# The front of a fused FNet and ELU kernel: first batch loaded tile by tile, two folds on GpSimd, and the channel-128 rows moved to earlier steps

## The chip, the cores and the metric

One NeuronCore of a Trainium2 chip runs the kernel. The metric is device time in microseconds for one execution, lower is better; the figures of the kernel before are three runs and one profiled execution.

## The reference

```python
def _attn_ref(x):                      # x: (8, 3008, 256) float32
    X = np.fft.fft(x, axis=1)
    X = np.fft.fft(X, axis=2)
    return X.real.astype(np.float32)

def _moe_ref(x, w_in, w_out):          # x: (24064, 256), w_in: (256, 2048), w_out: (2048, 256)
    h = x @ w_in
    g = np.where(h > 0.0, h, np.exp(np.minimum(h, 0.0)) - 1.0)
    return (g @ w_out).astype(np.float32)
```

The output of the first feeds the second. The two weight matrices arrive as 64-bit floats, so the kernel converts them itself.

## The kernel before, in words

**The sequence transform.** A batch is four tiles `xl0` to `xl3` of 128 rows by six blocks of 256 channels: `xl0` and `xl3` hold rows in rising order, `xl1` and `xl2` mirrored rows. Each is filled half by gathers that GpSimd issues (`gather`) and half by plain DMAs in SP's queue (`ahead`, `back`). `fold_x` adds and subtracts mirrored channels (`e0` to `e3`, `o0` to `o3`), then mirrored rows (`E0`, `E2`, `O0`, `O2`, `EO0` to `EO3`, `S`/`D`). DFT matrices `MC` turn the folded tiles into four half transforms of a batch (R and I, even and odd), which VectorE unfolds and joins into the rings `Rr` and `Ir`. Rings and the later stages work in column tiles of 256; there are 47 of them.

**The layers.** For each column tile there are eight steps, so 376 in all, of `PERIOD` = 4.8 model units. Step s does P (`mm_P`: `Wc` by `Rr`), V (`even_part`: VectorE adds the outer product of row `Rb` and column `wex`), Q (`mm_Q`: `Ws` by `Ir`), then h, the relu and exp on ScalarE (b+, b-, x+, x-) and g+, g- on VectorE. Two steps later the products with `w_out` follow: directly (`mm_plain`) for the first 16 steps, and from step 16 as seven products on sums that GpSimd makes (`sum_1` to `sum_4`). Finished tiles are combined, transposed on VectorE (`turn_u`, `turn_v`) and stored by SP in many small DMAs (`store`, L1199). All of an engine's compute runs in the order of its instructions, so an engine that waits holds up what stands behind it.

**Weights.** `w1_chunks` and `w2_chunks` are loaded raw and converted by steps named in the schedule (`w0a`, `w0b`, `w0R` and so on, on VectorE, ScalarE and GpSimd). `fold_chunk` (`f0`) turns a chunk of `w_in` into `Wc` and `Ws`. For chunks 2 to 7 the last row of `Ws` is written to DRAM (`wx`, L525) and read back as the columns `wex` (L528), both by SP.

**Channel 128.** It pairs with no other channel, so its rows come apart. Batch 0 takes them from the loaded tiles (`fold_first`, `dft_ext_0`); for all eight batches at once, `load_ext` fetches single elements (16 calls, L809), `sort_ext` orders them on ScalarE, `xe_dr` and `get_ext` (L839, L844) take them through DRAM into the tile `xs`, `fold_ext` folds them on GpSimd, and `dft_ext` transforms them. `ext_side` copies the results to SBUF, `ext_unfold` and `ext_rows` unfold and join them, and DMAs write them to DRAM, whence `spread_ext` brings them into `Rb` and into row 127 of `Ir`.

**The order.** Every piece of work is an event `at(t, fn)`. Events are sorted by time and traced in that order; instructions that go through `pin` keep it on their engine, other DMAs are placed by the framework's scheduler. The list `FRONT` gives the events of the start by name.

Of the kernel before, what the change touches and what calls it, by code (L numbers as in the profile page):

```python
# [9 lines left out]
FP = mybir.dt.float32  # L10
# [5 lines left out]
ALU = mybir.AluOpType  # L16
# [5 lines left out]
HALF = SEQ // 2  # L22
# [3 lines left out]
NE = 377  # L26
NO = 376
NA = (95, 94)
# [102 lines left out]
def kernel(  # L131
# [313 lines left out]
    def load_mats(ri, kodd, cuts=()):  # L445
        n = OFF[2 * ri + kodd]
        ends = (0, *cuts, BW[kodd])
        for a, z in zip(ends, ends[1:]):
            nc.sync.dma_start(
                out=MC[ri, kodd][:, a:z], in_=MC_dr.ap()[:, n + a : n + z]  # L450
            )
# [29 lines left out]
    def vtt(o, a, b, op):  # L481
        pin(nc.vector.tensor_tensor(out=o, in0=a, in1=b, op=op))  # L482
# [214 lines left out]
    def steps_of(pos, n, step):  # L697
        stop = pos + (n - 1) * step + (1 if step > 0 else -1)
        return slice(pos, stop if stop >= 0 else None, step)
# [7 lines left out]
            yield steps_of(pos, m, step), i, i + m  # L707
            i += m

    def unfold(es, even, near, ab, ri, kodd, M, tt):  # L710


        na, nc_ = NA[kodd], NC[kodd]
        n = NO if kodd else NE
        a, c = even[0:M, 0:na], even[0:M, 2 * na : 2 * na + nc_]
        b, ab = near[0:M, 0:na], ab[0:M]
        tt(ab[:, 0:na], a, b, ALU.add)
        p, q = (b, a) if ri else (a, b)
        tt(ab[:, steps_of(nc_ - 1, 94, -1)], p[:, 0:94], q[:, 0:94], ALU.subtract)
        tt(es[0:M, 0:nc_], ab[:, 0:nc_], c, ALU.add)  # L720
        p, q = (c, ab) if ri else (ab, c)
        tt(es[0:M, steps_of(n - 1, 188, -1)], p[:, 0:188], q[:, 0:188], ALU.subtract)

    def join(es, odd, kodd, to, tt, ri=0, part=None):


        def put(up, at, n, step, e, o):
            for sl, i, z in to(at, n, step):
                u, v = (e, o) if up or not ri else (o, e)
                tt(sl, u(i, z), v(i, z), ALU.add if up else ALU.subtract)  # L730

        def run(t, start, step):
            return lambda i, z: t[:, steps_of(start + i * step, z - i, step)]

        base, top = kodd * RUN, kodd * RUN + RUN - 1
        for up in (True, False):
            if part not in (None, up):
                continue
            if kodd:
                put(up, base if up else top, NO, 1 if up else -1, run(es, 0, 1), run(odd, 0, 1))  # L740
                continue
            for h in range(2):
                first = h if up or h else 2
                n = (189, 188)[h] if up else (187, 188)[h]
                put(
                    up,
                    base + first if up else top - first + 1,
                    n,
                    2 if up else -2,
                    run(es, first, 2),  # L750
                    run(odd, 189 * h + first // 2, 1),
                )

    class Dft:
# [21 lines left out]
        def unfold(self):  # L776
            self.es = spool.tile([128, NE], FP, tag="bs", bufs=3, name="bs")
            ab = spool.tile([128, 189], FP, tag="ab", bufs=2, name="ab")
            unfold(self.es, self.even, self.near, ab, self.ri, self.kodd, self.M, vtt)

        def to(self, at, n, step):
            for sl, i, z in ring_cut(self.b * HALF + at, n, step):
# [99 lines left out]
    def ext_side(g, rows=NB):  # L882
        kodd, par = EXT[g]
        n = (NO if kodd else NE) if par else 2 * NA[kodd] + NC[kodd]
        t = spool.tile([128, 380], FP, tag="side", bufs=2, name="side")
        act(t[0:rows, 0:n], state["ext"][32 * g : 32 * g + rows, 0:n])
        state["side", par] = t

    def ext_unfold(kodd, tt, rows=NB):
        even = state["side", 0]  # L890
        a = spool.tile([128, NE], FP, tag="bs", bufs=3, name="bs")
        ab = spool.tile([128, 189], FP, tag="ab", bufs=2, name="ab")
        unfold(a, even, even[:, NA[kodd] : 2 * NA[kodd]], ab, 0, kodd, rows, tt)
        state["es"] = a[0:rows]

    def ext_rows(kodd, tt, rows=NB):
        if not kodd or rows < NB:
            rx = spool.tile([128, HALF + 1], FP, tag="rx", bufs=1, name="rx")
            state["rx"] = rx[0:rows]
        rx, a, b = state["rx"], state["es"], state["side", 1][0:rows]  # L900
        base = kodd * RUN

        def to(at, n, step):
            yield rx[:, steps_of(at, n, step)], 0, n

        join(a, b, kodd, to, tt)
        if not kodd:
            tt(rx[:, HALF:], a[:, 0:1], b[:, 0:1], ALU.subtract)
            nc.sync.dma_start(
                out=r4_dr.rearrange("o b -> b o"), in_=rx[:, HALF : HALF + 1]  # L910
            )
        nc.sync.dma_start(
            out=r128_dr[0:rows, base : base + RUN], in_=rx[:, base : base + RUN]
        )

    def spread_ext(b, kodd):
        for sl, a, z in ring_cut(b * HALF + kodd * RUN, RUN, 1):
            a, z = a + kodd * RUN, z + kodd * RUN
            nc.sync.dma_start(
                out=Rb[:, sl],  # L920
                in_=r128_dr[b : b + 1, a:z].to_broadcast([128, z - a]),
            )
            nc.sync.dma_start(out=Ir[127:128, sl], in_=r128_dr[b : b + 1, a:z])
# [68 lines left out]
    def exp_neg(ap):  # L992
        act(ap, ap, func=AF.Exp, scale=-1.0)
# [273 lines left out]
    L_first, loads = load_x(0)  # L1267
    row_table(1)
    loads[0]()
    loads[6]()  # L1270
    w1_chunks[0].load()
    row_table(0)
    row_table(2)
    for load in loads[1:6] + loads[7:]:
        load()
    row_table(3)
    exp_neg(warm)
    nc.sync.dma_start(out=CC, in_=CC_dr.ap())
    load_mats(0, 0, (663,))
    w1_chunks[1].load()  # L1280
    nc.sync.dma_start(out=pick, in_=PK_dr.ap())
    EO, ops = fold_x(
        L_first,
        lambda key: nc.vector,
        lambda key, n: (0, 4, n) if key in ("e0", "e2") else (0, n),
    )

    def dft_now(d, par, tag):
# [7 lines left out]
    def at(t, fn):  # L1296
        events.append((t, len(events), fn))


    def load_rest():  # L1300

        ops["x1", 0]()
        act(MC[1, 0][0:1, 0:1], L_first[1][0:1, 0:1])
        load_mats(1, 0)
        w2_chunks[0].load()
        w1_chunks[2].load()
        load_mats(0, 1)
        for chunk in (w1_chunks[3], w2_chunks[1], w1_chunks[4], w2_chunks[2]):
            chunk.load()
        load_mats(1, 1)  # L1310
        w1_chunks[5].load()
        w2_chunks[5].load()
# [21 lines left out]
        ("R4", R_even.half),  # L1334
    )}
    for (key, i) in list(ops):
        names[key + "ab"[i] if key in ("e0", "e2") else key] = ops[key, i]
    for c in range(6):
        for name, chunk in ((f"w{c}", w1_chunks[c]), (f"u{c}", w2_chunks[c])):
            for key, fn in zip(  # L1340
# [26 lines left out]
    for slot in range(8):  # L1367
# [7 lines left out]
            names[f"{key}{slot}"] = lambda fn=fn, i=i: fn(i)  # L1375

    FRONT = (
        (-20.84, "e3 o3"),
        (-19.11, "w0a w0b w0p w0R c3"),
        (-17.62, "w0s w0M"),  # L1380
        (-16.21, "e0a e2b o2"),
        (-14.32, "e2a o0 c2"),
        (-12.89, "E2 f0 O2"),
        (-11.63, "xl1 xs e1 x-even"),
        (-9.8, "e0b c1 o1 c0 x-odd x-copy Wc0"),
        (-8.58, "E0 Ws0 EO0 S0 D0"),
        (-7.29, "wm0 wex0 O0 R-odd"),
        (-5.76, "w1b EO2 S2 D2"),
        (-4.55, "w2b R-even u0b w2d u0a EO1 w1d"),
        (-3.25, "I-odd R-copy w1l w1a x-sum u0l"),  # L1390
        (-1.92, "w1R R-sum w1p I-even x-down R-up"),
        (-0.64, "Irc2 w1s u0p P0 x-up I-copy w1M"),
        (0.82, "R-down O-even Irc I-sum u1l V0"),
        (2.21, "w1P w2l P1 I-up u0d"),
        (3.48, "I-down Q0 u0R R4 V1"),
        (4.76, "f1 h0 b+0 O-copy u0s Q1"),
        (5.99, "x+0 w2a b-0 u0M O-odd"),
        (7.24, "Wc1 g+0 x-0 O-sum Ws1"),
# [159 lines left out]
    at(9 * T + 4.75, dft_ext_0)  # L1558
    for g in (2, 3):
        at(10 * T + 1.46, lambda g=g: ext_side(g, 1))  # L1560
    at(11 * T + 3.54, lambda: ext_unfold(1, gtt, 1))
    at(11 * T + 3.55, lambda: ext_rows(1, gtt, 1))
    at(11 * T + 3.6, lambda: spread_ext(0, 1))
    for n in range(16):
        at((10.2 + 0.7 * n) * T, lambda n=n: load_ext(*divmod(n, 4)))
    at(24 * T + 1.5, sort_ext)
    at(26 * T, get_ext)
    at(32 * T + 1.35, fold_ext)
    at(32 * T + 4.75, dft_ext)
    at(33 * T + 1.46, lambda: ext_side(0))  # L1570
    at(33 * T + 1.47, lambda: ext_side(1))
    at(35 * T + 0.2, lambda: ext_unfold(0, vtt))
    at(35 * T + 1.5, lambda: ext_rows(0, vtt))
    at(35 * T + 4.75, lambda: ext_side(2))
    at(35 * T + 4.76, lambda: ext_side(3))
    at(36 * T + 0.2, lambda: ext_unfold(1, vtt))
    at(36 * T + 1.5, lambda: ext_rows(1, vtt))
    fold_keys = [(k, p) for k in FOLDS for p in range(2 if k[0] not in "cxSD" else 1)]
    n_big = sum(k[0] not in "cxSD" for k, _ in fold_keys)
    for b in range(1, NB):  # L1580
# [82 lines left out]
```

## Time and profile before

| what | value |
|---|---|
| median of 3 runs | 1961.19 us (1960.39 to 1961.99) |
| profiled execution, its own time | 1964.17 us |
| its span | 1962.4 us |
| mean granted TensorE clock | 0.994 |
| TensorE, VectorE, ScalarE, GpSimd busy | 98%, 67%, 44%, 72% |
| instructions | 27279 |
| DMA | 262111 packets, 69.70 MB, 245375 packets under 512 B |

TensorE (PE) is nearly always busy. The useful views are therefore those of its few idle stretches: what it waited for, and what its feeder was doing. In a line of the time line the first two figures are the start and the busy time in microseconds; `xN` merges N instructions, and a bracket gives the idle time before and what ended it. Merged lines give no single duration.

### The profile page before, as it was taken

To read this page: it belongs to the slowest core of one execution; us is meant where nothing else is said; L and a number is where in the kernel's file an instruction comes from. 1 tells how busy PE (TensorE), PEld (TensorE's weight loads), DVE (VectorE), ACT (ScalarE), POOL (GpSimd) and SP (SyncE) were. 2 spreads that over 40 slices of the span, in tenths; PEclk is the share of its full clock that TensorE was granted. 3 is DMA by queue.
4 is the path that set the end of the run, shared out by engine and by line. 5 is a ranking of instruction groups with operands and counts; after the bars stand their busy time and mean duration, and the time that the engine had idled before them with its cause. 6 is when DMAs were issued, how large, how long until landed. Compare 5 with 4: busy or idle time off the path is not lost.

```text
span 1962.4 us, 27279 instructions
## 1 busy us (share of the span) xinstructions
PE 1929.7 (98%) x8912; PEld 1655.8 (84%) x8912; DVE 1310.3 (67%) x2517; ACT 864.3 (44%) x1678; POOL 1403.9 (72%) x1868
## 2 busy tenths in 40 slices
PE   7899999999999999999999999999999999999998
PEld 4678878888888888888888888888888888888887
DVE  7766676667666666666666666666666666667665
ACT  3554434444444444444444444444434444344443
POOL 3687767777677776787677776778767787456565
PEclk9999999999999999999999999999999999999999
DMA  9244121120111112011110102102020110100101
GB/s 287 75 21 48 22 55 21 26 47 16 45 18 34 33 23 49 15 40 23 30 43 20 38 18 45 28 19 51 13 49 17 20 20 16 17 11 12 22 11 23
DMA packets 262111, 69.70 MB, mean 36 GB/s; under 512 B 245375, under 2 KB 246291, under 8 KB 261969
## 3 DMA queue, kind: packets, MB, share of 16 engines
q1 hardware_dynamic: 255952, 55.11, 15.1%
q0 software_dynamic: 3840, 12.59, 2.1%
q8 instruction: 71, 1.16, 0.3%
q14 instruction: 72, 0.58, 0.1%
q10 hardware_dynamic: 2176, 0.26, 0.1%
HBM read 43.07 MB, written 24.80 MB: 35 GB/s over the span
## 4 chain that ended last, share of the span: by engine, by line
PE 93%; DVE 4%; DMA 1%; POOL 1%; issue 1%; SPq 0%; ACT 0%; DVEq 0%; POOLq 0%
PE H L476 37%; PE pB L476 16%; PE pC L476 16%; PE pD L476 16%; PE pA L476 8%; DVE E L968 1%; DVE G L998 1%; POOL G L485 0%; DMA xl<-in_x_dram 0%; DMA CC<-chan_mats 0%; DVE v L482 0%; DVE bs L482 0%; DVE e L573 0%; DMA wex<-wx 0%; DVE u L482 0%
## 5 line engine op out<-in xcount | busy, mean ns | idle before, releaser
L485 POOL TENSOR_TENSOR G<-G 128x256 f32<-128x256 f32 x1440 | 1036.8, 730 | 486.3 <-DVE G L998 378.1
L968 DVE SCALAR_TENSOR_TENSOR E<-Rb,wex,H 128x256 f32<-128x256 f32 x752 | 327.8, 477 | 535.7 <-PE H L476 521.1
L488 ACT ACTIVATE G<-H 128x512 f32<-128x512 f32 x376 | 224.6, 597 | 971.8 <-DVE G L982 961.1
L476 PE MATMUL H<-Ir,Ws 128*128 128x256 f32 x1504 | 390.0, 382 | 13.1 <-DVE E L968 12.2
L476 PE MATMUL H<-Rr,Wc 128*128 128x256 f32 x1504 | 387.6, 380 | 2.0 <-DVE Ir L482 1.4
L476 PE MATMUL pC<-G,WT 128*128 128x256 f32 x1440 | 370.4, 380 | 0.0
L476 PEld LDWEIGHTS H<-Ir,Ws 128*128 128x128 f32 x1504 | 279.2, 190 | 63.5 <-DVE E L968 17.7
L476 PEld LDWEIGHTS H<-Rr,Wc 128*128 128x128 f32 x1504 | 285.0, 190 | 53.0 <-issue 4.5
L476 PEld LDWEIGHTS pC<-G,WT 128*128 128x128 f32 x1440 | 274.2, 190 | 37.5
L982 DVE SCALAR_TENSOR_TENSOR G<-E,H 128x512 f32<-128x512 f32 x376 | 256.8, 683 | 43.2 <-POOL G L485 3.8
L998 DVE SCALAR_TENSOR_TENSOR G<-G,H 128x512 f32<-128x512 f32 x376 | 255.8, 680 | 43.5 <-ACT G L488 43.4
L998 DVE SCALAR_TENSOR_TENSOR G<-M,G 128x512 f32<-128x512 f32 x376 | 256.7, 683 | 1.6 <-ACT M L488 1.6
L488 ACT ACTIVATE G<-G 128x512 f32<-128x512 f32 x376 | 233.2, 620 | 0.0
L476 PE MATMUL pB<-G,w 128*128 128x256 f32 x784 | 232.5, 384 | 0.0
L476 PE MATMUL pD<-G,w 128*128 128x256 f32 x784 | 229.4, 379 | 0.0
L476 PE MATMUL pA<-G,w 128*128 128x256 f32 x784 | 229.3, 379 | 0.0
L488 ACT ACTIVATE M<-G 128x512 f32<-128x512 f32 x376 | 223.9, 596 | 3.3 <-DVE G L982 3.3
L488 ACT ACTIVATE M<-M 128x512 f32<-128x512 f32 x376 | 220.9, 588 | 0.1
L476 PE MATMUL pB<-G,WT 128*128 128x256 f32 x720 | 215.2, 380 | 1.0 <-POOL G L485 0.7
L476 PE MATMUL pD<-G,WT 128*128 128x256 f32 x720 | 214.7, 380 | 0.0
L476 PEld LDWEIGHTS pB<-G,w 128*128 128x128 f32 x784 | 151.3, 193 | 21.3
L476 PEld LDWEIGHTS pD<-G,w 128*128 128x128 f32 x784 | 149.2, 190 | 20.4
(170 smaller groups left out, 1442.3 us busy)
## 6 DMA issues: line engine op xcount, KB each, us to landing
out_dram<-ot SPq DMA_DIRECT2D x496, 32.0 KB
xl<-in_x_dram SPq DMA_DIRECT2D x16, 256.0 KB
xl<-in_x_dram SPq DMA_DIRECT2D x32, 128.0 KB
out_dram<-ot SPq DMA_DIRECT2D x256, 2.0 KB
Rb<-r SPq DMA_DIRECT2D x10, 376.0 KB
raw<-in_moe_w_in_dram SPq DMA_DIRECT2D x7, 512.0 KB
raw<-in_moe_w_out_dram SPq DMA_DIRECT2D x4, 512.0 KB
out_dram<-ot SPq DMA_DIRECT2D x64, 28.0 KB
```

The source lines that it names most:

```text
L476: nc.tensor.matmul(out_, lhsT=lhsT, rhs=rhs, start=start, stop=stop, skip_group_check=True)
L485: pin(nc.gpsimd.tensor_tensor(out=o, in0=a, in1=b, op=op))
L488: pin(nc.scalar.activation(out=o, in_=i, func=func, **kw))
L968: nc.vector.scalar_tensor_tensor(out=S.E[:, c], in0=Rb[:, cols(i)], scalar=wex[:, f : f + 1], in1=S.H[:, c], op0=ALU.mult, op1=ALU.add,)
L982: nc.vector.scalar_tensor_tensor(out=two(S.G[:, 0:512])[:, :, ::-1], in0=two(S.E), scalar=2.0, in1=two(S.H), op0=ALU.mult, op1=ALU.subtract,)
L998: nc.vector.scalar_tensor_tensor(out=o, in0=e, scalar=-1.0, in1=h, op0=ALU.add, op1=ALU.max)
```

## The change

Six edits. The first batch's SP loads are issued tile after tile; the first chunk of `w_in` is loaded behind the tiles, the DFT matrices and `CC`, and the second chunk with the rest. The folds `o1` and `O0` of batch 0 go to GpSimd, and the folds `e0` and `e2` are no longer cut in two. The first 18 lines of `FRONT` become ten with another order. Unfolding channel 128 is split into `unfold_near` and `unfold_far` and joining into up and down, each an event in a step of its own; batch 0's goes from GpSimd to VectorE. The channel-128 data is loaded at a closer spacing and sorted, fetched, folded and transformed in steps 18 to 20 instead of 24 to 32. The odd half's sides share one tile (`sides`), so that they last until steps 29 to 32.

```diff
--- before.py
+++ after.py
@@ -707,16 +707,19 @@
             yield steps_of(pos, m, step), i, i + m
             i += m
 
-    def unfold(es, even, near, ab, ri, kodd, M, tt):
+    def unfold_near(even, near, ab, ri, kodd, M, tt):
 
 
         na, nc_ = NA[kodd], NC[kodd]
-        n = NO if kodd else NE
-        a, c = even[0:M, 0:na], even[0:M, 2 * na : 2 * na + nc_]
-        b, ab = near[0:M, 0:na], ab[0:M]
+        a, b, ab = even[0:M, 0:na], near[0:M, 0:na], ab[0:M]
         tt(ab[:, 0:na], a, b, ALU.add)
         p, q = (b, a) if ri else (a, b)
         tt(ab[:, steps_of(nc_ - 1, 94, -1)], p[:, 0:94], q[:, 0:94], ALU.subtract)
+
+    def unfold_far(es, even, ab, ri, kodd, M, tt):
+        na, nc_ = NA[kodd], NC[kodd]
+        n = NO if kodd else NE
+        c, ab = even[0:M, 2 * na : 2 * na + nc_], ab[0:M]
         tt(es[0:M, 0:nc_], ab[:, 0:nc_], c, ALU.add)
         p, q = (c, ab) if ri else (ab, c)
         tt(es[0:M, steps_of(n - 1, 188, -1)], p[:, 0:188], q[:, 0:188], ALU.subtract)
@@ -776,7 +779,8 @@
         def unfold(self):
             self.es = spool.tile([128, NE], FP, tag="bs", bufs=3, name="bs")
             ab = spool.tile([128, 189], FP, tag="ab", bufs=2, name="ab")
-            unfold(self.es, self.even, self.near, ab, self.ri, self.kodd, self.M, vtt)
+            unfold_near(self.even, self.near, ab, self.ri, self.kodd, self.M, vtt)
+            unfold_far(self.es, self.even, ab, self.ri, self.kodd, self.M, vtt)
 
         def to(self, at, n, step):
             for sl, i, z in ring_cut(self.b * HALF + at, n, step):
@@ -882,30 +886,42 @@
     def ext_side(g, rows=NB):
         kodd, par = EXT[g]
         n = (NO if kodd else NE) if par else 2 * NA[kodd] + NC[kodd]
-        t = spool.tile([128, 380], FP, tag="side", bufs=2, name="side")
+        if not kodd or rows < NB:
+            t = spool.tile([128, 380], FP, tag="side", bufs=2, name="side")
+        else:
+            if not par:
+                state["sides"] = spool.tile([128, 776], FP, tag="xn", bufs=1, name="sides")
+            t = state["sides"][:, 380 * par : 380 * par + 380]
         act(t[0:rows, 0:n], state["ext"][32 * g : 32 * g + rows, 0:n])
-        state["side", par] = t
-
-    def ext_unfold(kodd, tt, rows=NB):
-        even = state["side", 0]
+        state["side", kodd, par] = t
+
+    def ext_near(kodd, rows=NB):
+        even = state["side", kodd, 0]
+        state["ab"] = spool.tile([128, 189], FP, tag="ab", bufs=2, name="ab")
+        unfold_near(
+            even, even[:, NA[kodd] : 2 * NA[kodd]], state["ab"], 0, kodd, rows, vtt
+        )
+
+    def ext_far(kodd, rows=NB):
         a = spool.tile([128, NE], FP, tag="bs", bufs=3, name="bs")
-        ab = spool.tile([128, 189], FP, tag="ab", bufs=2, name="ab")
-        unfold(a, even, even[:, NA[kodd] : 2 * NA[kodd]], ab, 0, kodd, rows, tt)
+        unfold_far(a, state["side", kodd, 0], state["ab"], 0, kodd, rows, vtt)
         state["es"] = a[0:rows]
 
-    def ext_rows(kodd, tt, rows=NB):
-        if not kodd or rows < NB:
+    def ext_rows(kodd, up, rows=NB):
+        if up and (not kodd or rows < NB):
             rx = spool.tile([128, HALF + 1], FP, tag="rx", bufs=1, name="rx")
             state["rx"] = rx[0:rows]
-        rx, a, b = state["rx"], state["es"], state["side", 1][0:rows]
+        rx, a, b = state["rx"], state["es"], state["side", kodd, 1][0:rows]
         base = kodd * RUN
 
         def to(at, n, step):
             yield rx[:, steps_of(at, n, step)], 0, n
 
-        join(a, b, kodd, to, tt)
+        join(a, b, kodd, to, vtt, 0, up)
+        if up:
+            return
         if not kodd:
-            tt(rx[:, HALF:], a[:, 0:1], b[:, 0:1], ALU.subtract)
+            vtt(rx[:, HALF:], a[:, 0:1], b[:, 0:1], ALU.subtract)
             nc.sync.dma_start(
                 out=r4_dr.rearrange("o b -> b o"), in_=rx[:, HALF : HALF + 1]
             )
@@ -1267,22 +1283,20 @@
     L_first, loads = load_x(0)
     row_table(1)
     loads[0]()
-    loads[6]()
-    w1_chunks[0].load()
     row_table(0)
     row_table(2)
-    for load in loads[1:6] + loads[7:]:
+    for load in loads[1:]:
         load()
     row_table(3)
     exp_neg(warm)
+    load_mats(0, 0, (663,))
     nc.sync.dma_start(out=CC, in_=CC_dr.ap())
-    load_mats(0, 0, (663,))
-    w1_chunks[1].load()
+    w1_chunks[0].load()
     nc.sync.dma_start(out=pick, in_=PK_dr.ap())
     EO, ops = fold_x(
         L_first,
-        lambda key: nc.vector,
-        lambda key, n: (0, 4, n) if key in ("e0", "e2") else (0, n),
+        lambda key: nc.gpsimd if key in ("o1", "O0") else nc.vector,
+        lambda key, n: (0, n),
     )
 
     def dft_now(d, par, tag):
@@ -1302,6 +1316,7 @@
         ops["x1", 0]()
         act(MC[1, 0][0:1, 0:1], L_first[1][0:1, 0:1])
         load_mats(1, 0)
+        w1_chunks[1].load()
         w2_chunks[0].load()
         w1_chunks[2].load()
         load_mats(0, 1)
@@ -1334,7 +1349,7 @@
         ("R4", R_even.half),
     )}
     for (key, i) in list(ops):
-        names[key + "ab"[i] if key in ("e0", "e2") else key] = ops[key, i]
+        names[key] = ops[key, i]
     for c in range(6):
         for name, chunk in ((f"w{c}", w1_chunks[c]), (f"u{c}", w2_chunks[c])):
             for key, fn in zip(
@@ -1375,24 +1390,16 @@
             names[f"{key}{slot}"] = lambda fn=fn, i=i: fn(i)
 
     FRONT = (
-        (-20.84, "e3 o3"),
-        (-19.11, "w0a w0b w0p w0R c3"),
-        (-17.62, "w0s w0M"),
-        (-16.21, "e0a e2b o2"),
-        (-14.32, "e2a o0 c2"),
-        (-12.89, "E2 f0 O2"),
-        (-11.63, "xl1 xs e1 x-even"),
-        (-9.8, "e0b c1 o1 c0 x-odd x-copy Wc0"),
-        (-8.58, "E0 Ws0 EO0 S0 D0"),
-        (-7.29, "wm0 wex0 O0 R-odd"),
-        (-5.76, "w1b EO2 S2 D2"),
-        (-4.55, "w2b R-even u0b w2d u0a EO1 w1d"),
-        (-3.25, "I-odd R-copy w1l w1a x-sum u0l"),
-        (-1.92, "w1R R-sum w1p I-even x-down R-up"),
-        (-0.64, "Irc2 w1s u0p P0 x-up I-copy w1M"),
-        (0.82, "R-down O-even Irc I-sum u1l V0"),
-        (2.21, "w1P w2l P1 I-up u0d"),
-        (3.48, "I-down Q0 u0R R4 V1"),
+        (-19.0, "e3 o3 c3"),
+        (-16.0, "e2 o2 c2 E2 O2"),
+        (-12.5, "e0 o0 c0"),
+        (-10.0, "xl1 xs e1 c1 o1 x-even O0 E0 x-odd x-copy EO0 S0 D0"),
+        (-7.0, "R-odd w0a w0b R-even w0p w0R R-copy w0s w0M"),
+        (-4.5, "f0 EO2 S2 D2 Wc0 R-sum I-odd R-up Ws0 I-even x-sum wm0 wex0"),
+        (-1.9, "x-down Irc2 P0 x-up Irc I-copy R-down w1b w1d w1l"),
+        (-0.6, "I-sum w1a P1 w1R w1p EO1"),
+        (0.8, "I-up V0 O-even w1s w1M R4 w2b u0b w2d u0a u0l"),
+        (2.3, "I-down Q0 w1P w2l u0p u0d V1 u1l u0R"),
         (4.76, "f1 h0 b+0 O-copy u0s Q1"),
         (5.99, "x+0 w2a b-0 u0M O-odd"),
         (7.24, "Wc1 g+0 x-0 O-sum Ws1"),
@@ -1558,23 +1565,33 @@
     at(9 * T + 4.75, dft_ext_0)
     for g in (2, 3):
         at(10 * T + 1.46, lambda g=g: ext_side(g, 1))
-    at(11 * T + 3.54, lambda: ext_unfold(1, gtt, 1))
-    at(11 * T + 3.55, lambda: ext_rows(1, gtt, 1))
-    at(11 * T + 3.6, lambda: spread_ext(0, 1))
+    for step, fn in (
+        (11, lambda: ext_near(1, 1)),
+        (11, lambda: ext_far(1, 1)),
+        (12, lambda: ext_rows(1, True, 1)),
+        (12, lambda: ext_rows(1, False, 1)),
+    ):
+        at(step * T + 4.25, fn)
+    at(12 * T + 4.3, lambda: spread_ext(0, 1))
     for n in range(16):
-        at((10.2 + 0.7 * n) * T, lambda n=n: load_ext(*divmod(n, 4)))
-    at(24 * T + 1.5, sort_ext)
-    at(26 * T, get_ext)
-    at(32 * T + 1.35, fold_ext)
-    at(32 * T + 4.75, dft_ext)
-    at(33 * T + 1.46, lambda: ext_side(0))
-    at(33 * T + 1.47, lambda: ext_side(1))
-    at(35 * T + 0.2, lambda: ext_unfold(0, vtt))
-    at(35 * T + 1.5, lambda: ext_rows(0, vtt))
-    at(35 * T + 4.75, lambda: ext_side(2))
-    at(35 * T + 4.76, lambda: ext_side(3))
-    at(36 * T + 0.2, lambda: ext_unfold(1, vtt))
-    at(36 * T + 1.5, lambda: ext_rows(1, vtt))
+        at((10.2 + 0.5 * n) * T, lambda n=n: load_ext(*divmod(n, 4)))
+    at(18 * T + 1.5, sort_ext)
+    at(19 * T, get_ext)
+    at(20 * T + 1.35, fold_ext)
+    at(20 * T + 4.75, dft_ext)
+    for g in range(4):
+        at((21 + g // 2) * T + (1.46, 3.3)[g % 2], lambda g=g: ext_side(g))
+    for step, fn in (
+        (22, lambda: ext_near(0)),
+        (23, lambda: ext_far(0)),
+        (24, lambda: ext_rows(0, True)),
+        (26, lambda: ext_rows(0, False)),
+        (29, lambda: ext_near(1)),
+        (30, lambda: ext_far(1)),
+        (31, lambda: ext_rows(1, True)),
+        (32, lambda: ext_rows(1, False)),
+    ):
+        at(step * T + 4.25, fn)
     fold_keys = [(k, p) for k in FOLDS for p in range(2 if k[0] not in "cxSD" else 1)]
     n_big = sum(k[0] not in "cxSD" for k, _ in fold_keys)
     for b in range(1, NB):
```

## The prediction

> **What bounds the kernel now.** I read the page first, then the chain and TensorE's waits, then the time lines of the queues around the edits.
>
> ```profile
> PE 1929.7 (98%) x8912; PEld 1655.8 (84%) x8912; DVE 1310.3 (67%) x2517; ACT 864.3 (44%) x1678; POOL 1403.9 (72%) x1868
> PE 93%; DVE 4%; DMA 1%; POOL 1%; issue 1%; SPq 0%; ACT 0%; DVEq 0%; POOLq 0%
> ```
>
> TensorE is busy 98% of the span and is 93% of the chain. The change adds and removes no matmul, so it can only move TensorE's idle time and the slow clock after it. From step 16 a step costs 4.75 us of matmuls; nothing from 265 us on is touched. What can move lies before.
>
> TensorE's waits, front included:
>
> ```profile
> PE H L476 <- DVE E L968: 12.2, 6, 5.2
> PE H L476 <- DMA CC<-chan_mats: 5.9, 1, 5.9
> ```
>
> Three stalls stand behind the first line. At 60 us `wex` of chunk 2 sits in SP's queue behind a weight load (5.2 us; not an edited place). At 132 us `wex` of chunk 7 is late, by the chain:
>
> ```profile
> 126.78 1.55 SPq L919
> ...
> 128.75 3.71 DMA wx<-Ws
> ...
> 132.47 2.04 DMA wex<-wx
> ...
> 135.54 2.08 PE H L476 x4
> ```
>
> TensorE waits 3.3 us there and then runs at a granted clock of 0.75. The third is the channel-128 work on VectorE at 242 to 255 us:
>
> ```profile
> 242.76 0.57 DVE L482 TENSOR_TENSOR ab<-side 8x95 f32<-8x95 f32 x2
> 243.36 1.57 DVE L482 TENSOR_TENSOR bs<-ab,side 8x189 f32<-8x189 f32 x2
> ...
> 245.64 2.04 DVE L482 TENSOR_TENSOR rx<-bs,side 8x189 f32<-8x189 f32 x5
> ...
> 250.64 0.94 DVE L482 TENSOR_TENSOR ab<-side 8x94 f32<-8x94 f32 x2 [0.54 <-ACT side L488]
> 251.62 1.30 DVE L482 TENSOR_TENSOR bs<-ab,side 8x188 f32<-8x188 f32 x2
> ...
> 253.62 0.99 DVE L482 TENSOR_TENSOR rx<-bs,side 8x376 f32<-8x376 f32 x2
> ```
>
> These 15 operations take 7.4 us in the steps that also combine tile 3. Between the P groups at 232.67 and 259.25 us lie four steps and one 1.12 us DFT, so 20.1 us of matmuls take 26.6: **6.5 us are lost**.
>
> The queue that the new plan leans on is SP's:
>
> ```profile
> 154.24 10.46 SPq L1199 DMA_DIRECT2D out_dram<-ot  x24
> 164.75 0.31 SPq L809 DMA_DIRECT2D x<-in_x_dram  x1
> 165.16 5.73 SPq L1199 DMA_DIRECT2D out_dram<-ot  x8
> 170.93 1.87 SPq L809 DMA_DIRECT2D x<-in_x_dram  x2
> 172.90 5.69 SPq L1199 DMA_DIRECT2D out_dram<-ot  x8
> 178.62 2.58 SPq L809 DMA_DIRECT2D x<-in_x_dram  x2
> ...
> 188.95 0.33 SPq L839 DMA_DIRECT2D xe_dr<-xp  x1
> ...
> 191.41 0.38 SPq L844 DMA_DIRECT2D xs<-xe_dr  x1
> ```
>
> From 154 to 181 us SP issues without a pause: the stores of tiles 0 and 1 take 0.44 and 0.71 us each to issue.
>
> **What the Trainium skill says.** "SBUF — State Buffer", section "SBUF: two separate sides": VectorE with two SBUF inputs and GpSimd share a port pair under an exclusive lock; the loser waits for the other's whole instruction. The trace agrees: the four 8-row `bs` operations of one size last from 335 to 1031 ns, the long ones beside a GpSimd operation. "TensorE: Matmul & The Clock Gate", section "What's actually happening": after an idle window of about 3.4 us the clock halves. The trace agrees roughly: even the 2.4 us wait at 251 us is followed by a clock of 0.72. "DMA: Bandwidth & Descriptors", section "Rules for kernel authors": a non-contiguous last dimension gives one descriptor an element. Between 132 and 154 us six `load_ext` of 1536 single elements are 9536 packets and fill 60% of 22 us: 2.2 us each.
>
> **Part 1, the front.** Removed: 0.52 MB of weights ahead of the tiles. About 3.8 MB move by 17.0 us, near 0.25 MB/us, so `xl0` comes in time by some 2 us, and VectorE's 4.5 us idle before 17.01 us shrinks. I let it start tile 2 at 11.8 us (the third gather's issue at 5.0 plus the median landing of 6.8). Six operations at 0.87 us end at 17.0. But the w0 chain (0.34+0.34+3x0.69 = 2.75 us), which filled idle time at 9.7 to 12.5 us, now stands in the busy stretch. The folds `o1` and `O0` leave VectorE (-1.9 us). On GpSimd a half of each took 1.18 and 1.00 us in the later batches, so 2.36 and 2.0 us whole; both engines read two SBUF tiles then, and by the lock VectorE loses up to 4.3 us. With that I get S0/D0 done at 25.2 us (27.3 before) and, adding the listed operations (w0 2.75, EO2/S2/D2 1.3, three unfolds 3.0, joins 2.8, w1a/w1b 0.7, EO1 0.9, V0 0.8), V0 done at 37.4 instead of 38.5. Q0 is then 1.7 us earlier, but w1s, w2b, u0b and u0a (1.7 us) are still to do on an engine that is 96% busy until 50 us. I take **0**. Ends: -3 if the lock hardly bites, +2 if a late tile or the cold clock stretches the first DFTs. Gathers, CC, MC and `pick` keep their cost; CC no longer limits anything, since f0 now waits for w0M.
>
> **Part 2, channel 128 of batch 0.** Its GpSimd operations (0.65+1.12+2.26 = 4.0 us at 120 to 124 us) become VectorE operations, two at a time in steps 11 and 12. GpSimd, 96% busy there, gains 4 us; each VectorE pair may wait 1.3 us for its lock, so the rows are ready at about 125.5 us instead of 124.3. SP then issues the row's store, the two spreads and chunk 7's `wx`. The three `load_ext` between go ahead of the row, so the tail shortens by about what the row is late; `wex` lands near 133 instead of 134.5 us. I take **-1.5**; ends -6.5 (the whole stall) and +1.
>
> **Part 3, channel 128 of the other batches: the VectorE operations.** Same work, two operations a step in steps 22 to 32, placed after h. VectorE idles 1.85 us there in each step ("<-PE H"), but GpSimd's four sums (3.04 us) run just then: a pair costs 0.6 to 1.6 us as above. Steps 29 to 31 also carry batch 1's unfold and join (1.2 to 1.4 us). So 6.5 us come back and some 1.5 are paid: **-5.0**, ends -6.5 and -3.
>
> **Part 4, the same data's way in.** Loads, sort, fold and DFT move from steps 10-24, 24, 32 and 32 to 10-18, 18, 20 and 20. P of step 16 is at 146.47 us (its first Winograd product, two steps on, at 157.70), of step 18 at 156.83, of 20 at 166.33.
>
> The last load falls at 17.7T, behind `turn_u(0)` at 17T+1: 12 of the 24 stores, 154.24+5.2 = 159.5 us. A load issued alone at 164.75 had landed 2.2 us later, so here near 162. The sort's turn on ScalarE is at 158.3 us. With its 1.36 us of six copies, exp of the minus half of step 17 comes at 163.3 instead of 158.1, its g at 164.5 instead of 160.6, and TensorE wants it at 162.4. Queued behind on ScalarE are the next step's relu and exp; VectorE waits in g with h and E behind it. That is a 2.1 us stall, and with about 1 us of slow clock **+3.1**; ends 0 and +6. The sort waits already before (1.36 us at 187.56) and costs nothing: the slack is near 3 us.
>
> `xe_dr` then queues behind the rest of tile 0's stores and tile 1's first eight: 154.24+10.46+0.3+5.8 = 170.8 us. `xs` follows 2.46 us later (188.95 to 191.41 before), 173.3. Its packets end near 195.2, 3.8 us after issue; beside stores I add 0.7: **177.8 us**. The fold is due on GpSimd at 168.1, or 171.2 after the sort's stall, and lasts 1.3 us; behind it in order stand the sums of step 19. They start at 179.1 instead of 172.1, less some 1.5 us of slack: a stall of 5.5 us, plus 2.5 of slow clock (the 5.2 us stall at 60 us cost 7.7 in all). **+8.0**; ends 0 (the queue empties in time) and +15 (the second half of tile 1's stores, 5.7 us, also lies ahead of `xs`). `dft_ext`, due 3.4 us later, hides in this wait. Two more sides at once hold one of three H banks for two steps; TensorE needs two: 0.
>
> **Sum:** 0 - 1.5 - 5.0 + 3.1 + 8.0 = +4.6 us. The profiled execution took 1964.17 us (span 1962.4), 3.0 above the median of the runs, 1961.19; the same edit gives 1968.8 for it and 1965.8 for the median. A measurement of this kernel can tell 0.2%, 3.9 us, from no change.
>
> **Rivals.** *The queue is in time, faster.* If `xs` lands before about 170 us and the last load before 161, Part 4 costs nothing: -6.5, 1954.7 us. It decides in SP's queue between 154 and 175 us: for it speaks that stores and loads are ordered by a plan I don't see; against it 10.46+5.73 us of stores that are all due earlier. *The lock hardly bites and the order of SP's queue drops the 60 us stall*: -3 and -7.7 on the sum, about 1955. *The two halves cancel, no change*: the sort costs nothing and the fold waits half as long, 4 us, about 1958.7 to 1962. *Tile 1's other stores come first*: +5.7 on the sum, 1971.5. *The new front order does not act* because landings, not order, set it: Part 1 stays 0 and nothing else moves.
>
> **Numbers.** Late sort and fold 0.52 (a third of it with the extra stores), cancelling 0.22, either faster case 0.26. So 1965.8 us, faster 0.26, same 0.22, slower 0.52. The faster case's ends (Part 1 at -3, Part 2 further down) reach to 1952, the slower ones with a further queue stall to 1977.
>
> **What would show it.** Right: `xp<-x` near 160 us with ScalarE idle 2 to 4 us before it; POOL `xs<-xs` near 178 with an idle of 5 or more put to a DMA, and a TensorE wait of 4 to 6 us just after; no TensorE wait at 240 to 258; VectorE operations of 1.5 us or more beside `o1` and `O0`. Wrong: POOL `xs<-xs` without idle before it, or Q0 earlier by 4 us with dense matmuls after.

## The result, and the profile after

The changed kernel took **1974.51 us** in the median of four runs (1972.17 to 1976.37), the kernel before 1961.59 beside it: ratio 1.0064, 95% interval 1.0047 to 1.0082. It is slower, as forecast, by 12.9 us instead of 4.6. Its profiled execution took 1972.17 us (span 1970.3). That one is 2.3 us below the median of its kernel and the profiled one of before 2.6 above its own, so the two traces show 8 us of the 12.9 (3.1 us of the rest can be the clock behind one wait, see batch 0 and chunk 7's `wex` below).

The page's busy times and chain first:

```profile
PE 1930.3 (98%) x8912; PEld 1656.5 (84%) x8912; DVE 1320.1 (67%) x2519; ACT 865.0 (44%) x1678; POOL 1404.6 (71%) x1864
PE 91%; DVE 3%; DMA 2%; POOL 1%; SPq 1%; issue 1%; ACT 0%; DVEq 0%; POOLq 0%
```

TensorE does the same work (8912 matmuls, 1930.3 us); DMA and SP's queue have come into the chain. TensorE's waits:

```profile
PE H L476 <- DVE E L984: 9.4, 4, 4.8
PE pC L476 <- DVE xe L482: 8.1, 1, 8.1
PE pA L476 <- DVE G L1014: 7.7, 1, 7.7
PE pA L476 <- issue: 3.1, 1, 3.1
PE H L476 <- POOL raw L485: 1.7, 1, 1.7
PE H L476 <- POOL xe L485: 1.4, 1, 1.4
```

The waits for `E` fell from 12.2 to 9.4 us in total: those at 240 to 254 us are gone, those at 60 and 132 us stay (4.8 and 3.2). New are one of 7.7 us for `g` at the sort, one of 1.4 for the fold, and two in the front: 1.7 for chunk 1's `raw`, and 3.1 that ends at 39.45 us, just after VectorE's fold `EO1` (39.35). The 8.1 us before the first DFT stand in place of the wait for `CC`. Now SP's queue around the channel-128 data (start, time over which it issues, instructions):

```profile
131.07 0.47 SPq L928 DMA_DIRECT2D r<-rx  x1
135.04 0.36 SPq L935 DMA_DIRECT2D Rb<-r  x1
...
138.49 19.47 SPq L813 DMA_DIRECT2D x<-in_x_dram  x9
158.06 7.96 SPq L1215 DMA_DIRECT2D out_dram<-ot  x12
166.07 0.35 SPq L813 DMA_DIRECT2D x<-in_x_dram  x1
166.52 10.15 SPq L1215 DMA_DIRECT2D out_dram<-ot  x20
176.76 0.39 SPq L843 DMA_DIRECT2D xe_dr<-xp  x1
178.92 1.30 SPq L1215 DMA_DIRECT2D out_dram<-ot  x3
180.33 0.40 SPq L848 DMA_DIRECT2D xs<-xe_dr  x1
```

Nine loads in a row take 2.16 us each to issue on average; one alone takes 0.35. The first stores, whose tile VectorE has transposed at 156.83 us (first line below), begin at 158.06, take 0.66 us each instead of 0.44, and the last load stands behind twelve of them. What that does on the engines, from their time lines:

```profile
156.12 0.71 DVE L1162 STREAM_TRANSPOSE ot<-pA 128x512 f32<-128x512 f32 x1
...
170.26 1.35 ACT L488 ACTIVATE xp<-x 32x192 f32<-32x192 f32 x6 [9.44 <-DMA out_dram<-ot]
...
172.87 1.22 PE L476 MATMUL pA<-G,w 128*128 128x256 f32 x2 [7.65 <-DVE G L1014]
...
184.58 0.39 POOL L485 TENSOR_TENSOR xs<-xs 128x96 f32<-128x96 f32 x1 [4.44 <-DMA xs<-xe_dr]
```

ScalarE stands 9.44 us before the sort; the exp behind it in ScalarE's order starts at 171.52, as the six copies end, and TensorE stands 7.65 us for the `g` made from it. The fold on GpSimd stands 4.44. The sort's wait is put down to a store's landing although no data go from a store to `xp`. I read it as: loads and stores in SP's queue up to 166 us decide it; which of the last ones released it is an inference of the trace.

A ledger by the start of each step's P group, run minus before (profiled executions, us). `dft_ext` itself, 2.1 us of matmuls, moved from behind step 32 to an earlier step; until step 33 that is in the numbers. Each column is one execution, and executions of the same code differ: up to step 12 "the rest alone" is the kernel before, and stands at -1.3 and -2.5. A difference of that size between two columns shows nothing by itself.

| step | after | new front alone | the rest alone | folds back | loads 0.45 | fetch on ScalarE | best version |
|---|---|---|---|---|---|---|---|
| 2 | +5.8 | +5.3 | -1.3 | +3.1 | +5.2 | +4.8 | -1.5 |
| 12 | +5.1 | +4.7 | -2.5 | +3.1 | +4.7 | +4.2 | -9.3 |
| 19 | +2.6 | +1.7 | -5.2 | +1.9 | +4.7 | +4.8 | -14.7 |
| 22 | +16.8 | +1.7 | +8.9 | +15.8 | +16.2 | +8.8 | -14.7 |
| 32 | +17.3 | +2.0 | +9.3 | +16.2 | +16.7 | +9.3 | -7.4 |
| 37 | +8.7 | +3.2 | +0.8 | +7.6 | +8.1 | +0.7 | -15.7 |

From the first column: front +5.1; batch 0's pieces and chunk 7's `wex` -2.5 (+0.7 at step 13, then -3.2); sort +10.1 (step 19 to 20); fold +4.1 less 2.1 of DFT, so +2.0; VectorE pieces -8.6 plus the 2.1, so -6.5, and +0.4 in their new steps. Sum +8.7; of that 0.8 comes back behind the last P group.

### The profile page after: what moved, and what is told of

Read it like the earlier page. It is cut to its first block, busy times and chain, and to the rows that moved or that the text cites. A ratio compares the mean times of both kernels' runs of the same rounds, so it can differ in the third digit from the quotient of the medians.

```text
span 1970.3 us, 27285 instructions
## 1 busy us (share of the span) xinstructions
PE 1930.3 (98%) x8912; PEld 1656.5 (84%) x8912; DVE 1320.1 (67%) x2519; ACT 865.0 (44%) x1678; POOL 1404.6 (71%) x1864
## 4 chain that ended last, share of the span: by engine, by line
PE 91%; DVE 3%; DMA 2%; POOL 1%; SPq 1%; issue 1%; ACT 0%; DVEq 0%; POOLq 0%
PE H L476 36%; PE pC L476 16%; PE pB L476 16%; PE pD L476 16%; PE pA L476 8%; SPq L813 1%; POOL G L485 1%; DVE E L984 1%; DVE G L1014 1%; DMA x<-in_x_dram 0%; DMA xl<-in_x_dram,ix 0%; DVE v L482 0%; POOL xl L211 0%; DVE G L998 0%; DVE rx L482 0%
## 5 line engine op out<-in xcount | busy, mean ns | idle before, releaser
L476 PEld LDWEIGHTS pA<-G,w 128*128 128x128 f32 x784 | 149.1, 190 | 28.4 <-DVE G L1014 8.1
```

The costliest lines, as they stand in the source:

```text
L476: nc.tensor.matmul(out_, lhsT=lhsT, rhs=rhs, start=start, stop=stop, skip_group_check=True)
```

## The experiments

Each median is beside that of the kernel before on the same chip (1961.2 us for runs 1, 2, 3 and 6, 1962.1 to 1962.3 for the others).

**1. The new front alone.** The kernel before with the new load order, `FRONT` and `o1`, `O0` on GpSimd.

> The kernel before with the changed front alone (load order, uncut e0/e2, o1 and O0 on GpSimd, new first ten lines of FRONT); channel 128 as before. Theory A, the loss is local to each stretch: matching the P groups of the two traces, the changed kernel is 5.8 us behind at step 2 and 5.1 us from step 5 on, so this kernel is 5 us over the one before (4 to 6.5), with step 2's P near 50 us instead of 44.5. Theory B, the front costs nothing and all of the loss comes from the sort and the fold of channel 128: within 2 us of the kernel before.

1968.53 us, ratio 1.0039 [1.0025, 1.0053]. Step 2 is 5.3 us later. Theory B is out; the median's 7.3 us is more than theory A's 4 to 6.5.

**2. The rest alone.** The changed kernel with the front of before.

> The changed kernel with the front of before; channel 128 as changed. Theory A (losses add up stretch by stretch): -2.5 at step 15, +10.1 at step 20, +2.0 at step 21 (net of the DFT that only moves), +0.4 at step 28 and -6.5 at steps 33 to 37, so +3.5 us over the kernel before (2 to 6), with ScalarE idle some 9 us ahead of the sort's copies. Theory B (the front costs nothing): 8 us or more over the kernel before.

1964.50 us, 1.0022 [1.0015, 1.0030]. The waits of 7.7 us at the sort and 1.5 at the fold are there without the new front. The two halves give +7.3 and +3.3, 10.6 of the 12.9: they add up within the scatter.

**3. The two folds back on VectorE.**

```diff
-        lambda key: nc.gpsimd if key in ("o1", "O0") else nc.vector,
+        lambda key: nc.vector,
```

> The changed kernel with o1 and O0 on VectorE instead of GpSimd; nothing else. Theory A (shared port lock): the long xa (2.12 us) and xd (1.76 us) shrink to 0.16 us, which gives 3.6 us back, and two folds of 0.87 us come on top, so P of step 2 is 1.8 us earlier than in the changed kernel and the whole run 1 to 2 us faster than it. Theory C (only the order of the weights' conversion matters): the folds' 1.7 us are added, the run is 0 to 2 us slower than the changed kernel.

1970.02 us, 1.0047 [1.0030, 1.0064]: 4.5 us less than the changed kernel, more than theory A's 1 to 2; the two intervals touch, so the total alone doesn't decide. Step 2 is earlier by 2.7. The lines of VectorE and GpSimd in the changed kernel show how work that left VectorE cost it time:

```profile
18.04 2.12 DVE L482 TENSOR_TENSOR xa<-xl,xl 128x6 f32<-128x6 f32 x1
...
20.27 1.76 DVE L482 TENSOR_TENSOR xd<-xa,xg 128x6 f32<-128x6 f32 x1
...
17.94 2.19 POOL L573 TENSOR_TENSOR o<-xl 128x768 f32<-128x768 f32 x1 [7.34 <-ACT MC L488]
20.21 1.80 POOL L573 TENSOR_TENSOR o<-o,o 128x768 f32<-128x768 f32 x1
```

Two operations on six elements a partition end when the folds on GpSimd end. With the folds back, the first reads

```profile
18.02 0.16 DVE L482 TENSOR_TENSOR xa<-xl,xl 128x6 f32<-128x6 f32 x1
```

The two folds take 1.9 us on VectorE and cost it 3.6 on GpSimd, about 1.7 us net.

**4 and 5. What else the front lost: two attempts.** Each is on top of 3 alone. Run 4 has chunk 1's conversion earlier, beside chunk 0's; run 5 has chunk 0 loaded and converted in the gap behind the first tile, as in the old order. The cuts show where the names go; the rows that they leave are not shown.

```diff
-        (-7.0, "R-odd w0a w0b R-even w0p w0R R-copy w0s w0M"),
+        (-7.0, "R-odd w0a w0b w1b w1a R-even w0p w1d w1l w1p w0R R-copy w0s w0M w1R w1s w1M"),
...
```

> The changed kernel with o1 and O0 back on VectorE and, in addition, the conversion of the second chunk of w_in (w1b, w1a, w1d, w1l, w1p, w1R, w1s, w1M) moved up in FRONT beside that of the first chunk, and w1P to the head of its row. Compare with the run that only brought the two folds back (step 2 at +3.10 us against the kernel before, 2.7 us of TensorE wait on the GpSimd product raw of chunk 1). Theory A, what is left of the front's loss is the late conversion of chunk 1: the wait of TensorE on raw is gone, step 2 starts 1.5 to 2.7 us earlier than in that run (+0.4 to +1.6), total 1967.5 to 1968.5. Theory B, it is the late even DFT of the row 128-sums (x-even at 22 us, cold clock) and VectorE being full until 45 us: conversion work moved up pushes S/D and the unfolds back by the same amount, step 2 unchanged or later (+3 to +5), total 1970 to 1972.

```diff
     loads[0]()
+    loads[6]()
+    w1_chunks[0].load()
...
-        (-19.0, "e3 o3 c3"),
+        (-19.0, "e3 o3 w0a w0b w0p w0R c3"),
+        (-17.6, "w0s w0M"),
...
```

> The changed kernel with o1 and O0 on VectorE and, in addition, the first chunk of w_in loaded ahead of the tiles again and its conversion put back behind the first tile's folds (w0a w0b w0p w0R after o3, then w0s w0M); the rest of the new front stays. In the run with the two folds back VectorE stood idle for 3.4 us before tile 2's first fold (12.80 us), did the w0 chain at 24.0 to 26.8 us, and was then never idle by more than 1.3 us until 50 us; step 2 was 3.1 us later than in the kernel before. Theory A, the rest of the front's loss is these 2.75 us of VectorE work, which the old order did while it waited for tiles: step 2 comes 1.5 to 2.75 us earlier, +0.3 to +1.6 against the kernel before, total 1967 to 1968.5. Theory B, the 0.52 MB ahead of the tiles delay their landing (and S0/D0) by as much as the gap hides: S0/D0 done 2 us later, step 2 unchanged or later (+2.6 to +4.5), total 1969.5 to 1971.5.

1970.77 us (1.0042 [1.0028, 1.0056]) and 1969.64 us (1.0042 [1.0029, 1.0054]); step 2 at +4.5 and +3.3 against +3.1 in run 3. By the totals theory B holds in both. The traces say less, because the first fold behind those of the first tile (`e3`, `o3`), on which the front hangs, does not start at the same time in all executions. In the seven traces with the new load order, where it is tile 2's, it starts between 12.80 us (run 3) and 14.84 (run 6), at 14.16 in run 4, and at 14.44 in run 5. Counted from that fold, P of step 2 begins after

| front | us |
|---|---|
| old front (six traces) | 27.5 |
| new, folds on GpSimd (five traces) | 36.4, once 37.5 (the changed kernel) |
| run 3 | 34.8 |
| run 4 | 34.8 |
| run 5 | 33.4 |

So run 3's gain is 1.6 us against four of the five, as its 1.7 net has it. Run 4 is theory B: the wait for `raw` goes, step 2 follows V0 (V of step 0) by 2.7 us less than in run 3, and V0 follows `S0`/`D0` by 2.7 us more. Run 5 is open: the conversion in the gap is worth 1.4 us, nearly theory A's 1.5, but tile 2 comes 1.6 us later than in run 3 and takes it back (`S0`/`D0` at 25.7 us instead of 24.1). Whether the 0.52 MB ahead of the tiles delayed it or this is the scatter, one trace can't tell. **Some 3 us of the front's loss stay unexplained by a run.** They lie behind V0: from its end to step 2 it is 6.0 us with the old front, 9.9 in run 3 and 9.7 in run 5. The trace of 3 offers the wait for `raw` (2.7 us) and two operations of w_out's conversion beside GpSimd's work (1.50 and 0.95 us; 0.42 each in the kernel before, at 30 us, when GpSimd had nothing to do); neither was tried alone.

**6. The sort three steps later**, fetch in 22, fold and DFT in 24, the pieces in steps 26 to 32 and 36.

> The changed kernel with the sort at step 21, its fetch at 22, fold and DFT at 24, sides at 25 and 26 and the eight VectorE pieces at steps 26 to 32 and 36; loads at the same spacing. Theory A (ScalarE and GpSimd stand idle because SP's queue is late): no ScalarE idle ahead of the sort and no GpSimd idle ahead of the fold, 12 us faster than the changed kernel (10 to 13), so 3 us below the kernel before. Theory D (the wait comes along because the loads or the stores, not the place, set it): less than 6 us faster than the changed kernel, with an idle ahead of the sort or the fold still in the trace.

1967.07 us, 1.0032 [1.0019, 1.0045]: 7.4 us less than the changed kernel, between theory A's 10 to 13 and theory D's less than 6. ScalarE no longer stands before the sort, and steps 16 to 24 keep one offset (+3.8). But the fold waits 6.89 us:

```profile
182.06 0.39 SPq L843 DMA_DIRECT2D xe_dr<-xp  x1
182.56 9.19 SPq L225 DMA_DIRECT2D xl<-in_x_dram  x2
191.84 0.54 SPq L848 DMA_DIRECT2D xs<-xe_dr  x1
...
198.08 0.39 POOL L485 TENSOR_TENSOR xs<-xs 128x96 f32<-128x96 f32 x1 [6.89 <-DMA xs<-xe_dr]
```

Between the fetch's two halves stand two loads of batch 2, and the second waits 8.0 us until GpSimd has made a fold (`o`) and its buffer is free. Another cause for the same wait: whatever stands ahead in the one queue.

**7. The loads closer**, at 0.45 steps instead of 0.5, so that the last one leaves the stores behind it.

> The changed kernel with the 16 load_ext at a spacing of 0.45 instead of 0.5 steps, so that the last load of them no longer stands behind the 12 first stores of tile 0 in SP's queue. Theory A, the sort's wait is the backlog of SP's queue, 2.16 us a load for nine loads in a row and 0.66 us a store behind them: ten loads in a row end near 160 us, the last one lands near 164 instead of 169.5, ScalarE idles 3 to 4 us before xp<-x instead of 9.4, TensorE waits 2 to 3 us there instead of 7.7, and 4 to 6 us come back of the total (1968.5 to 1970.5), unless the fold then waits for as long as the sort did (fetch behind the stores: 2 to 4 us of it). Theory B, the landing is set by the DMA engines and not by the order of issue (bytes in flight drain at their own pace): xp<-x stays within 1.5 us of 170.3 and the total within 1.5 us of the changed kernel.

1972.46 us, 1.0056 [1.0035, 1.0077]. Theory A is right on the sort and the total hardly moves:

```profile
158.96 17.00 SPq L1215 DMA_DIRECT2D out_dram<-ot  x32
176.06 0.39 SPq L843 DMA_DIRECT2D xe_dr<-xp  x1
...
164.91 1.36 ACT L488 ACTIVATE xp<-x 32x192 f32<-32x192 f32 x6 [1.99 <-DMA out_dram<-ot]
...
182.36 0.38 POOL L485 TENSOR_TENSOR xs<-xs 128x96 f32<-128x96 f32 x1 [7.57 <-DMA xs<-xe_dr]
```

The sort is 5.4 us earlier, the fetch is issued 0.7 us earlier, and the fold stands for what the sort no longer does. Sort and fold are one chain behind 32 stores; the wait moves from the one to the other, and of the 14.2 us that steps 19 to 22 lose in the changed kernel 11.5 are lost here.

**8. The fetch out of SP's queue**, on top of 7.

```diff
-        nc.sync.dma_start(out=xe_dr.rearrange("j b r -> (j b) r"), in_=t)
+        pin(nc.scalar.dma_start(out=xe_dr.rearrange("j b r -> (j b) r"), in_=t))
```

and the same for `xs<-xe_dr`.

> The run with the loads at 0.45 steps, with one more edit: the two DMAs of the fetch (xe_dr<-xp and xs<-xe_dr) are issued by ScalarE, in its order, and no longer by SP behind the stores. In that run the copies xp<-x were done at 166.3 us but xe_dr<-xp was issued at 176.06, behind 32 stores, and the fold stood 7.57 us. Theory A, the fetch waits for its place in SP's queue: it is now issued at 166.4 and about 171 us, xs lands near 175, when the fold is due (174.8): the fold's idle falls to 0 to 2 us and the total by 6 to 9 us, to 1963.5 to 1966.5. Theory B, it is the DMA engines that are full of the stores' packets, whatever queue the fetch stands in: the fold still stands 5 us or more, total within 2 us of 1972.5.

1965.30 us, 1.0018 [1.0010, 1.0026], 7.2 below run 7, as theory A had it:

```profile
166.42 0.36 ACTq L843 DMA_DIRECT2D xe_dr<-xp  x1
168.84 0.43 ACTq L848 DMA_DIRECT2D xs<-xe_dr  x1
175.42 0.39 POOL L485 TENSOR_TENSOR xs<-xs 128x96 f32<-128x96 f32 x1
```

No bracket stands behind `xs<-xs`: the fold no longer waits. The stores still run beside it, so it was the place in the queue and not the load on the DMA engines.

**9. The stall at 60 us**, untouched by the change: the kernel before, with one load pinned.

```diff
+            self.keep = lambda ins: ins
...
-            nc.sync.dma_start(
+            self.keep(nc.sync.dma_start(
...
+    w2_chunks[6].keep = pin
```

For all other chunks `keep` does nothing. In the kernel before, SP's queue at this place reads as follows; the third line's load waits 6.3 us for GpSimd's `raw`.

```profile
53.06 0.22 SPq L525 DMA_DIRECT2D wx<-Ws  x1
53.45 0.39 SPq L285 DMA_DIRECT2D raw<-in_moe_w_in_dram  x1
60.23 0.39 SPq L285 DMA_DIRECT2D raw<-in_moe_w_out_dram  x1
60.71 0.42 SPq L528 DMA_DIRECT2D wex<-wx  x1
```

> The kernel before with one edit: the load of the seventh piece of w_out is pinned to its place in the order, so that the scheduler does not put it on SP's queue between the store wx and the read wex of chunk 2 (it waits there for a buffer that GpSimd frees at 60 us). Theory A, head-of-line blocking of SP's queue is the whole cause of the 5.2 us stall at 60 us: it goes with its slow clock, 5 to 7.7 us less than the kernel before (1953.5 to 1956.5), and every later step is earlier by that. Theory B, wex of chunk 2 is late anyway by its own chain (row of Ws late from GpSimd), and the stall only changes its name: within 2 us of the kernel before.

1953.34 us, 0.9954 [0.9937, 0.9971]. `wex` follows `wx` after 1.1 us instead of 7.7, and no TensorE wait is left at 50 to 70 us:

```profile
52.17 0.22 SPq L527 DMA_DIRECT2D wx<-Ws  x1
52.57 0.39 SPq L286 DMA_DIRECT2D raw<-in_moe_w_in_dram  x1
53.28 0.39 SPq L530 DMA_DIRECT2D wex<-wx  x1
```

**10 to 12. Toward a better version.** First: the old front, the pinned load, and the channel-128 code of the change with loads from step 13.1 on at 0.5 steps, sort in 24, fold in 27, pieces in 29 to 32 and 35 to 38.

> The kernel before with its own front, the changed channel-128 code, but its events where their data is in time: loads from step 13.1 on at 0.5 steps (behind the row of chunk 7), sort in step 24 as in the kernel before, fetch in 26, fold and DFT in 27, sides in 28 and 29, the VectorE pieces one a step in 29 to 32 and 35 to 38; and the load of the seventh piece of w_out pinned as in the other run. Theory A, the parts add: -6.5 (VectorE pieces out of the combining steps) -2.5 to -6 (wait for wex of chunk 7 shorter or gone) -5 to -7.7 (stall at 60 us) +0 (sort and fold in time): 14 to 20 us below the kernel before, 1941 to 1947. Theory B, the pieces' cost is only moved to whichever step they stand in, or the fold waits again behind loads of the next batch: 5 to 9 us below, 1952 to 1956.

1957.89 us, 0.9975 [0.9966, 0.9984]: worse than the pin alone, and above the ranges of both theories. The last loads stood behind stores until 176.4 us, ScalarE idled 9.94 us before the sort, and TensorE 8.0. Then the loads at 0.3 steps, and the four sides in one step:

```diff
-        at((13.1 + 0.5 * n) * T, lambda n=n: load_ext(*divmod(n, 4)))
+        at((13.1 + 0.3 * n) * T, lambda n=n: load_ext(*divmod(n, 4)))
...
-        at((28 + g // 2) * T + (1.46, 3.3)[g % 2], lambda g=g: ext_side(g))
+        at(28 * T + (1.46, 1.47, 3.3, 3.31)[g], lambda g=g: ext_side(g))
```

> The combination run before it (old front, pinned weight load, channel-128 events in steps 24 to 38) with two edits: the load_ext from step 13.1 on at 0.3 steps instead of 0.5, so that they stand ahead of most stores, and all four sides copied in step 28 instead of two each in 28 and 29. There the sort stood 9.9 us for loads that were issued behind stores until 176.4 us (TensorE 8.0), and TensorE 2.5 us for the copies of the odd sides. Theory A, order in SP's queue: the last load is issued before 165 us, the sort does not wait, both stalls go: 9 to 13 us below that run, 1944 to 1949, and 4 to 9 below the run with the pinned load alone. Theory B, loads in a row push the stores and the fetch back by as much: the fold waits instead, total 1953 to 1958.

**1946.30 us, 0.9920 [0.9895, 0.9945]**, the best version, 28 us below the changed kernel and 16.0 below the kernel before, of which the pinned load alone gives 8.8 (run 9). The sort does not wait; the fold still does, 4.3 us (TensorE 3.1). The row of chunk 7, which no load precedes any more, goes through at once:

```profile
116.65 0.23 SPq L930 DMA_DIRECT2D r<-rx  x1
117.88 0.34 SPq L937 DMA_DIRECT2D Rb<-r  x1
118.28 0.27 SPq L941 DMA_DIRECT2D Ir<-r  x1
118.61 0.24 SPq L527 DMA_DIRECT2D wx<-Ws  x1
120.84 0.38 SPq L530 DMA_DIRECT2D wex<-wx  x1
```

From `r` to `Rb` 1.2 us here, 4.0 in the changed kernel. Last, the cure of run 8 on top of this:

> The last combination run (loads from step 13.1 on at 0.3 steps) with the two DMAs of the fetch issued by ScalarE, xs<-xe_dr one step after the sort. There xe_dr<-xp was issued at 183.44 us and xs<-xe_dr at 187.51, behind stores and behind loads of batch 2, though the sort was done at 173.1; the fold on GpSimd stood 4.3 us and TensorE 3.1 us. Theory A, the place in SP's queue again: xs lands before 182 us, the fold does not wait, 4 to 6 us less: 1940.5 to 1942.5. Theory B, something else holds step 28 (the DFT and four copies of sides at once): total within 1.5 us of 1946.3.

1950.40 us, 0.9938 [0.9922, 0.9955], slower by 4.1. Both theories miss the total. The fold no longer waits, as theory A had it, but now ScalarE does. From the chain of this run:

```profile
179.13 1.65 DMA out_dram<-ot
180.86 0.36 ACTq L845
181.27 0.59 ACT M L490
```

ScalarE had the copies done at 174.3 but issued `xe_dr<-xp` at 180.86, when a store landed, and stood for 6.95 us (TensorE 5.0). In run 8 the same instruction was issued at once. No data join the store to it; what it waited for stays open.

## Why the prediction was right, and where it was not

The direction and the leading mechanism held: sort and fold moved ahead of their data in SP's queue cost more than the spreading of the VectorE pieces gave (run 2). The result also lies in the range, but 1952 to 1977 us holds a gain as well as a loss, so that says little. Sort and fold together cost 12.1 us where 11.1 were forecast, and most of the miss is the front. By its parts:

- **Front, 0 (-3 to +2): wrong, +5.1.** The step that failed is the sum on VectorE. `S0`/`D0` were done at 26.0 us (forecast 25.2), with tile 2 first folded at 12.8 instead of 11.8. V0, forecast for 37.4, ended at 40.7, 14.7 us after `S0`/`D0` instead of 12.2. The lock was priced at "up to 4.3" and measured 3.6 at the two folds, so that was not the error. But it was counted only beside `o1` and `O0`: at 37 us it also stretches `EO1`'s operation (2.05 us, 0.95 alone), and VectorE stands 1.3 us for `anti`, which the sum didn't have; these two are nearly all of the 2.5 us. Behind V0 the GpSimd part of chunk 1's conversion, which begins at 37.24 us instead of 32.30, was given no price: TensorE waits 1.7 us for it.
- **Batch 0 and chunk 7's `wex`, -1.5 (-6.5 to +1): -2.5, by luck.** The pieces now on VectorE cost 0.7 us (TensorE waits 1.15 us at 126 us, 0.48 before). The wait for `wex` stayed 3.2 us (3.3 before). What was gained is 3.1 us of clock behind that wait: the first group of matmuls took 1.13 us instead of 2.08. Run 1, which has the channel-128 code of before, gains the same there:

```profile
141.21 1.13 PE L476 MATMUL H<-Ir,Ws 128*128 128x256 f32 x4 [3.17 <-DVE E L984]
...
140.33 1.13 PE L476 MATMUL H<-Ir,Ws 128*128 128x256 f32 x4 [3.32 <-DVE E L968]
```

  The first line is the changed kernel, the second run 1. Run 4, with the changed code, waits 3.13 us and takes 2.07 for the group. So this is a difference of executions and not the change's; without it the ledger ends at +11.8, near the 12.9 of the medians. The three loads did go ahead of the row, as forecast; overlooked was that the row's store then lands late: 4.0 us from `r` to `Rb`, against 1.2 in run 11, where no load stands before it.
- **VectorE pieces, -5.0 (-6.5 to -3): -6.5, and +0.4 paid.** All that was lost came back. No TensorE wait is left at 225 to 285 us, as forecast; in their new steps, where VectorE waits for h, the pieces cost next to nothing.
- **Sort, +3.1 (0 to +6): +10.1, outside its ends.** The mis-sized term is the landing of the last load, "near 162"; the sort began at 170.3. It was worked from stores that start at 154.24 and take 0.44 us each, as before; but nine loads ahead of them now took 19.47 us, at the 2.2 us that the prediction itself had read for a load and did not add into the queue. Of the difference 2.6 us is no loss of the sort's: all of the kernel was that much later by then, the sort's own turn too (160.8 instead of 158.3). The stores then stood 1.2 us for the loads, twelve of them took 7.96 us instead of 5.2, and the last load was followed by the sort after 4.2 us instead of 2.2.
- **Fold, +8.0 (0 to +15): +2.0.** `xs` landed at 184.5, not 177.8, but the sort's stall had moved the fold's turn to 180.1. The two numbers were for one chain and shouldn't have been worked apart. Run 7 shows the forecast picture (sort idle 2.0, fold 7.6), at nearly the same total.
- The stall at 60 us stayed, so that rival is out; run 9 shows its cause. "The queue is in time" fell at 154 to 180 us, the place that it was to be decided.

The skill's lock ("SBUF — State Buffer", section "SBUF: two separate sides") is borne out by run 3. On the clock ("TensorE: Matmul & The Clock Gate", section "What's actually happening") the page calls the window free-running, so that a change of clock depends on where in it the matmuls fall. These runs agree that a wait near its length has no one price: 3.2 us at the same place cost nothing more in the changed kernel, and 3.3 us cost 3.1 more in the kernel before. The prediction's 0.75 and 0.72 are means over stretches that were slow in part; the granted clock was 0.50 from 135 to 141 us, and for 3.4 us behind the wait at 251 us.

## What to carry to other kernels

Before moving a step earlier, list its queue item by item, each with its measured issue time when the queue is backed up, not when idle, and put a load ahead of the stores that it would otherwise follow. Work a chain of waits as one sum: an improvement at its first wait reappears at the next until the last transfer is earlier. An engine that looks idle is not a free place for work if it holds up a busy one through a shared port.

## What had not been expected of the hardware

- A DMA of 1536 single elements takes 0.35 us to issue alone and 2.16 on average in a row of nine; a store behind them 0.66 instead of 0.44. SP's queue then becomes a time line of its own, longer than the engines' plan.
- A VectorE operation on six elements a partition, 0.16 us alone, lasted 2.12 us beside one GpSimd operation of 2.19.
- Moving a DMA to another engine's queue frees it from the stores ahead (run 8) but that engine can then stand: 6.95 us in run 12, put down to a store's landing, cause open.
